# Attention and a squared-ReLU FFN on one core: who computes the low parts of x, a third buffer for the words of w_in, and three sums put off

## The chip, the cores and the metric

One core of a Trainium2 chip runs the whole kernel. The metric is device time in microseconds (us). A run is one execution; the time given is the median of three runs. The profile is of one further execution.

## The reference

```python
rmsnorm = lambda x, g: x / np.sqrt(np.mean(x * x, -1, keepdims=True) + 1e-6) * g
# q, k, v: (8, 12, 448, 64), float32
scores = 1 / np.sqrt(64) * np.matmul(rmsnorm(q, g_q), rmsnorm(k, g_k).transpose(0, 1, 3, 2))
attn = np.exp(scores - scores.max(-1, keepdims=True))
attn = attn / (attn.sum(-1, keepdims=True) + 1e-9)
x = np.matmul(attn, v).transpose(0, 2, 1, 3).reshape(3584, 768)
h = x @ w_in                      # w_in: (768, 2048), float64 in memory
r = np.maximum(h, 0.0)
out = (s * (r * r) + b) @ w_out   # w_out: (2048, 768), float64 in memory
```

## The kernel before, in words

**Two stages.** The first stage does the attention of all 8 batches and, beside it, the product x @ w_in with the ReLU. The second does the square, the affine step and the product with w_out, by a scheme of Strassen's kind with 7 products for each group of 256 tokens; `multiply(n)` is one product, 24 matmuls of 128x384, and `n = 7 * g + k` is its number for group `g`.

**Slots.** Two heads make a pair; there are 48 pairs, six to a batch. The order of the first stage is written by hand: the program walks through numbered slots, eight to a pair, 384 in all. In slot `s_` TensorE does the score tile that the exponential needs (`score_t`, tile `st`, two matmuls, L405 and L408), the score tile of ten slots later from which the row maxima are taken (`score`, tile `sh`, L367), and the product of the weights with v of two slots earlier (`weigh`, tile `av`, L464). Three `filler(2)` put six matmuls of x @ w_in (tile `ph`, L177) between them. A slot starts here with its L405 matmul. Work off TensorE is put into slots by `at(slot, function, ...)`; functions in the tuple `late` are recorded after the row maximum of the slot, the others before. Every engine then works through its own list in order, and so does SP, which issues all of the DMAs.

**Splitting.** Most matmul operands are split into a high part in the matmul's own type and a low part, the difference to it. `exponent` and `split_e` run on ScalarE, `split_e_lo` (tile `al`, or the upper half of `ah`) on VectorE. `split_kq` casts ka and qa on ScalarE and takes the differences (L351, L352) on GpSimd in the next slot; `scale` (L329 GpSimd, L330 VectorE) stands two slots ahead of it. `score` needs the new ka three slots after `split_kq` began.

**x and the boundary between batches.** When a pair is done, `divide` makes its tile `u` on GpSimd (L510). `split_x(b, g)` turns the six u of batch b into the tiles x0 to x5, high part on ScalarE (L517) and low part on VectorE (L518), one buffer per g. The matmuls of x @ w_in for batch b start at the end of slot 48(b+1)+8, so the slots around 48(b+1)+9 are called a boundary here; batch 0 has no such matmuls to run beside.

**Words of w_in.** w_in is loaded as 24 pieces of 512 float64 words (`load_piece`, tile `w64`, two buffers) and turned into single precision by five `convert` steps per piece on VectorE (L128 to L136), ScalarE (L129, L147) and GpSimd (L149). The tuple `PACE` gives the slot in which the conversion of each piece starts: every sixth slot up to 55, then every second or third up to 84. The second convert step is the last that reads the words.

**Second stage.** The seven combined blocks of w_out are loaded and split in chunks (`split_chunk`), the sums of the r tiles (`sum1` to `sum4`) and the splits of the operands (`split`) go to VectorE, and their tiles come from a list of free units.

Of the kernel before, what the change touches and what calls it, by code (L numbers as in the profile page):

```python
# [9 lines left out]
F32 = mybir.dt.float32  # L10
F32R = mybir.dt.float32r
I32 = mybir.dt.int32
AF = mybir.ActivationFunctionType
ALU = mybir.AluOpType
# [9 lines left out]
START = 9  # L24
# [9 lines left out]
TURNED = 10  # L34

PLAIN = 10

PACE_OUT = tuple(48 * b + 16 + 8 * i for b in range(2, 8) for i in range(4))

# [4 lines left out]
def attention_then_relu2_ffn(  # L44
# [29 lines left out]
    nc = tc.nc  # L74
    V, S, G, T = nc.vector, nc.scalar, nc.gpsimd, nc.tensor

    NPAIR, P, _, SEQ = kq.shape
# [5 lines left out]
    NP = NPAIR // B  # L83
    H = 2 * NP
    TILES = 2 * SEQ // P
    NV = PLAIN
    NQ = 4
    QC = SEQ // NQ
    REST = SEQ % P
    NCC = DM // P  # L90
# [5 lines left out]
    WI = 512  # L96
    NH = NFC // 2
    NQ3 = HALF // P
    W = 8
# [109 lines left out]
    with tc.tile_pool(name="apool", bufs=1) as ap:  # L209
        raws, kqs, invs, vrs, nmxs, shs, tks = ({} for _ in range(7))  # L210
        sts, movers, avs, uzs, zts, zbs, us = ({} for _ in range(7))
# [180 lines left out]
        def chunk(i):  # L392
            p, g = divmod(i, W)
            j, kc = divmod(g, NKC)
            return p, j, kc, P if kc < 3 or p < NV else REST
# [38 lines left out]
        def split_e_lo(i):  # L434
            p, j, kc, rows = chunk(i)
            if p < NV:
                return
            st, bank = sts.pop(i)
            ah = movers[i][0]
            if kc < 3:  # L440
                al = ap.tile([P, SEQ], F32R, tag="al", bufs=2, name=f"al{i}")
                movers[i].append(al)
            else:
                al = ah[rows:]
            V.tensor_tensor(al, st[:rows, :SEQ], ah[:rows].bitcast(F32), ALU.subtract)  # L445
            free.append(bank)
# [65 lines left out]
        xs = {}  # L512

        def split_x(b, g):
            u = us.pop(b * NP + g)
            x = xs[b, g] = xp.tile([P, 2, SEQ], F32R, tag=f"x{g}", name=f"x{b}_{g}")
            S.copy(x[:, 0, :], u)  # L517
            V.tensor_tensor(x[:, 1, :], u, x[:, 0, :].bitcast(F32), ALU.subtract)  # L518

        def pieces():  # L520
            for i, (hi, lo, src) in enumerate(parts_of_w_in()):
                w = ap.tile([P, WI, 2], I32, tag="w64", bufs=2, name=f"w64i{i}")


                def words(i=i):
                    return ap.tile([P, WI], I32, tag="wa", bufs=3, name=f"wai{i}")

                yield load_double((w, words, hi), hi, lo, src)
# [50 lines left out]
                    of.bitcast(F32).rearrange("p (k n) -> p k n", k=4),  # L579
                )  # L580

        late = (convert, invert, convert_out)

        fill = iter(())

# [8 lines left out]
        def at(s_, f, *a):  # L594
            jobs[s_].append((f, a))
# [31 lines left out]
            at(s0 + 18 - soon, divide, p, 3)  # L627
        for b in range(B):
            for g in range(NCC):
                at(W * NP * (b + 1) + START - 2 + g, split_x, b, g)  # L630
        for s_ in (-18, -10):
            at(s_, load_piece)
        for i, s_ in enumerate(PACE):
            for n in range(5):
                at(s_ + n, convert, i, n)
            at(s_ + 3, load_piece)
        for i, s_ in enumerate(PACE_OUT):
            at(s_ - 4, load_out, i)
            for n in range(5):
# [11 lines left out]
        with tc.manual_schedule(engines=ORDERED):  # L651
            begun = []
            for s_ in range(FIRST, NSLOT + START + NCC):
# [17 lines left out]
                for f, a in jobs[s_]:  # L671
                    if f in late:
                        continue
                    g = f(*a)
# [18 lines left out]
                b, m = divmod(s_ + 1 - START, W * NP)  # L693
# [7 lines left out]
    with tc.tile_pool(name="opool", bufs=1) as op:  # L701
# [17 lines left out]
        def release(*us):  # L719
            units.extend(tag for _, tag in us if tag is not None)  # L720
# [10 lines left out]
        def split_chunk(i):  # L731
            k, c = divmod(i, 4)
            hi, lo = (x[:, 2 * c : 2 * c + 2] for x in combs[k])
            S.copy(hi, lo.bitcast(F32))
            (G if k == 6 else V).tensor_tensor(lo, lo.bitcast(F32), hi.bitcast(F32), ALU.subtract)

        NG = NT // (2 * P)
        As = [{} for _ in range(NG)]
# [45 lines left out]
        def sum4(g):  # L784
            combine(g, 4, As[g][0, 1], As[g][2], ALU.subtract)

        USES = ((0, 0), (0, 1), 2, 1, 3, 4, (1, 1))
        def split(n):
            g, k = divmod(n, 7)
            if g == NG:  # L790
                return
            u = As[g].pop(USES[k])
            hi, lo = halves[n] = spare.pop(n) if n in spare else (unit(f"hi{n}"), unit(f"lo{n}"))
            S.copy(hi[0], single(u))  # L794
            V.tensor_tensor(lo[0], single(u), single(hi), ALU.subtract)  # L795
            release(u)

        banks = {}

# [53 lines left out]
        with tc.manual_schedule(engines=ORDERED):  # L853
            early = {
                2: [(load_a, 0, *c) for c in QUADS],
                6: [(f, 0, *c) for c in QUADS for f in (square, affine)],
                7: [*((f, 0) for f in (sum1, sum3, sum2, split, sum4)), (split, 1), (split, 2)],
                10: [(split, 3)],
            }
            splits = {**{m: 2 * m - 2 for m in range(1, 7)}, 8: 12, 9: 14, 12: 16, 13: 18}  # L860
            loads = {2: 2, 6: 3, 10: 4}
            for i in range(8):
                load_chunk(i)
            for m in range(NFC - 2):
                filler(NCC * 3)
                keep_r()
                if m in loads:
                    for i in range(4):
                        load_chunk(4 * loads[m] + i)
                if m in splits:  # L870
                    for i in range(2):
                        split_chunk(splits[m] + i)
                for f, *a in early.get(m, ()):
                    f(*a)
                rectify()
            filler(None)
            rectify()
            keep_r()
            units.extend(f"x{c}" for c in range(NCC))
            splits = {1: 20, 2: 22, 4: 24, 5: 26}  # L880
            loads = {0: 5, 3: 6}
            for n in range(7 * NG):
                g, k = divmod(n, 7)
                if n in loads:
                    for i in range(4):
                        load_chunk(4 * loads[n] + i)
                multiply(n)
                if n:
                    settle(n - 1)
                if n > 1:  # L890
                    split(n + 2)
                if n in splits:
                    for i in range(2):
                        split_chunk(splits[n] + i)
                if g + 1 < NG:
                    if k in (1, 2):
                        for c in QUADS[2 * k - 2 : 2 * k]:
                            load_a(g + 1, *c)
                    if k in (2, 3):
                        for c in QUADS[2 * k - 4 : 2 * k - 2]:  # L900
                            square(g + 1, *c)
                            affine(g + 1, *c)
                    if k == 3:
                        sum1(g + 1)
                    if k == 4:
                        sum3(g + 1)
                        sum2(g + 1)
                    if k == 5:
                        sum4(g + 1)
                release(*halves.pop(n))  # L910
            settle(7 * NG - 1)


# [42 lines left out]
```

## Time and profile before

| | |
|---|---|
| three runs | 1430.03, 1432.8, 1439.4 us, median 1432.8 |
| profiled execution | 1433.59 us, its span 1431.8 |
| TensorE busy | 1390.2 us, 97% |
| VectorE, ScalarE, GpSimd busy | 1058.1, 880.5, 655.7 us |
| granted TensorE clock, mean | 0.993 |

The span is counted from the first to the last instruction. A window is a stretch of the span; its row gives the busy time and the number of instructions of each engine. A row of the timeline gives the start, the time that it took, engine, line and operation, and in brackets how long the engine had been idle and for what it waited. SPq rows are DMA issues. A busy VectorE or GpSimd includes time in which an instruction has started but is held up.

### The profile page before, as it was taken

Reading aid. Unit: us, or ns where it says so; the run is one execution under the profiler, and the core shown is the slowest. Engines: PE = TensorE matmul, PEld = TensorE weight load, DVE = VectorE, ACT = ScalarE, POOL = GpSimd, SP = SyncE. Lnnn points to the kernel's source line nnn. Section 1 sums busy time; section 2 is a strip of 40 time slices with the busy share of each in tenths; the row PEclk is TensorE's granted clock in tenths of the full one; section 3 lists DMA queues with packets and bytes.
Section 4 is the critical chain, followed back from the end, with each engine's and each line's share of the span. In section 5 each row is a group of like instructions: output and inputs, shape, how many; then the busy total and the mean of one; then the engine's idle time right before and its main releaser. Section 6 shows DMA issues by size and latency. Waiting matters only on the chain.

```text
span 1431.8 us, 21377 instructions
## 1 busy us (share of the span) xinstructions
PE 1390.2 (97%) x7024; PEld 1269.3 (89%) x7024; DVE 1058.1 (74%) x1603; ACT 880.5 (61%) x1586; POOL 655.7 (46%) x515
## 2 busy tenths in 40 slices
PE   6998999999999999999999999999999999999999
PEld 5666778899899889989989988999999999999998
DVE  6898897788788778788878878734686567766673
ACT  4887567777777777777777767645643444334431
POOL 7777787677577757767756765300020000000000
PEclk8999999999999999999999999999999999999999
DMA  4455686688678768778767876438733342334330
GB/s 130 131 148 158 191 245 187 183 245 234 192 225 246 209 192 244 223 199 236 239 197 223 243 214 187 148 101 275 239 85 94 105 124 83 92 89 127 99 87 34
DMA packets 257470, 247.07 MB, mean 173 GB/s; under 512 B 77968, under 2 KB 238736, under 8 KB 257360
## 3 DMA queue, kind: packets, MB, share of 16 engines
q1 hardware_dynamic: 257360, 245.71, 58.9%
q8 instruction: 56, 0.92, 0.3%
q14 instruction: 54, 0.44, 0.1%
HBM read 180.88 MB, written 53.40 MB: 164 GB/s over the span
## 4 chain that ended last, share of the span: by engine, by line
PE 81%; DVE 7%; ACT 4%; DMA 3%; issue 3%; POOL 2%; SPq 0%; POOLq 0%; DVEq 0%; ACTq 0%
PE p L808 28%; PE ph L177 27%; PE av L464 12%; PE sh L367 4%; PE st L405 4%; PE st L408 4%; DMA w64i<-in_dram 2%; DVE x L518 1%; DVE nmx L378 1%; ACT x L517 1%; PE tk L245 1%; ACT st L424 1%; DVE al L445 1%; DVE kq L330 1%; DVE ah L445 1%
## 5 line engine op out<-in xcount | busy, mean ns | idle before, releaser
L177 PE MATMUL ph<-x,wih 128*128 128x448 f32 x1536 | 491.9, 367 | 0.1
L177 PEld LDWEIGHTS ph<-x,wih 128*128 128x128 f32 x1536 | 290.0, 189 | 27.8 <-issue 4.9
L177 PE MATMUL ph<-x,wil 128*128 128x448 f32 x768 | 290.6, 378 | 0.0
L378 DVE TENSOR_REDUCE nmx<-sh 112x1 fp32r<-112x448 f32 x384 | 236.4, 618 | 65.3 <-PE sh L367 61.9
L424 ACT ACTIVATE st<-st 128x448 f32<-128x448 f32 (+1 forms) x304 | 159.6, 525 | 195.1 <-PE st L408 191.3
L464 PE MATMUL av<-ah,vs 128*128 128x448 f32 x608 | 174.8, 369 | 2.5 <-DVE al L445 2.5
L367 PE MATMUL sh<-ka,qa 128*112 128x448 f32 x384 | 149.2, 391 | 24.1 <-DVE ah L445 10.4
L405 PE MATMUL st<-qa,ka 128*128 128x448 f32 (+1 forms) x384 | 159.5, 415 | 3.5 <-DVE nmx L378 3.4
L432 ACT CAST ah<-st 128x448 fp32r<-128x448 f32 (+1 forms) x304 | 161.9, 532 | 1.6
L177 PEld LDWEIGHTS ph<-x,wil 128*128 128x128 f32 x768 | 144.6, 188 | 16.5 <-issue 4.9
L445 DVE TENSOR_TENSOR al<-st,ah 128x448 fp32r<-128x448 f32 x228 | 139.2, 611 | 23.4 <-ACT ah L432 22.7
L351 POOL TENSOR_TENSOR ka<-kq,ka 64x448 fp32r<-64x448 f32 x76 | 102.6, 1351 | 102.0 <-ACT ka L348 98.5
L367 PEld LDWEIGHTS sh<-ka,qa 128*112 128x112 f32 x384 | 107.7, 281 | 38.4 <-DVE ah L445 12.3
L408 PE MATMUL st<-qb,kb 128*128 128x448 f32 (+1 forms) x384 | 141.1, 368 | 0.0
L464 PEld LDWEIGHTS av<-ah,vs 128*128 128x128 f32 x608 | 113.6, 189 | 15.6 <-DVE al L445 5.4
L794 ACT CAST hi<-a 128x1024 fp32r<-128x1024 f32 x54 | 56.8, 1052 | 87.5 <-PE p L808 71.8
L352 POOL TENSOR_TENSOR qb<-kq,qa 64x448 fp32r<-64x448 f32 x76 | 100.0, 1316 | 5.7
L329 POOL TENSOR_TENSOR kq<-kq,rb 128x448 f32<-128x448 f32 x76 | 101.0, 1329 | 0.0
L510 POOL TENSOR_TENSOR u<-uz,zb 128x448 f32<-128x448 f32 x48 | 64.7, 1347 | 79.2 <-DMA zb<-z_d 75.2
L313 POOL TENSOR_TENSOR ri<-ri,mhalf 128x14 f32<-128x14 f32 x38 | 99.3, 2614 | 3.2
L298 POOL TENSOR_TENSOR vs<-vr,vs 128x512 fp32r<-128x512 f32 x38 | 56.9, 1498 | 82.7 <-issue 73.9
L795 DVE TENSOR_TENSOR lo<-s,hi 128x1024 fp32r<-128x1024 f32 x41 | 50.1, 1223 | 52.5 <-ACT hi L794 52.5
(238 smaller groups left out, 3084.4 us busy)
## 6 DMA issues: line engine op xcount, KB each, us to landing
kq<-in_dram SPq DMA_DIRECT2D x76, 448.0 KB, 5.2
rb<-i_d SPq DMA_DIRECT2D x76, 448.0 KB, 6.0
r_d<-r SPq DMA_DIRECT2D x128, 224.0 KB, 3.5
a<-r_d SPq DMA_DIRECT2D x48, 512.0 KB, 5.2
raw<-in_dram SPq DMA_DIRECT2D x38, 448.0 KB, 4.8
w64i<-in_dram SPq DMA_DIRECT2D x24, 512.0 KB, 4.6
w64o<-in_dram SPq DMA_DIRECT2D x48, 256.0 KB, 3.6
kb<-ka SPq DMA_DIRECT2D x96, 112.0 KB, 2.6
```

The costliest lines, as they stand in the source:

```text
L177: T.matmul(ph[:, :SEQ], w[:, cc, f0 : f0 + P], xs[b, cc][:, part, :], start=cc == 0 and m == 0, stop=cc == NCC - 1 and m == 2,)
L329: G.tensor_tensor(t[:, 0], t[:, 0], rb[:, 0], ALU.mult)
L351: G.tensor_tensor(ka[n][D:, a], t[D:, 0], ka[n][D:, a].bitcast(F32), ALU.subtract)
L367: T.matmul(sh[:QC, :SEQ], qa[p % 2][:, a].rearrange("k (p c) -> k c p", c=NQ)[:, c], ka[p % 2][:, a], start=True, stop=True,)
L378: V.tensor_reduce(out=nmxs[p][:, c : c + 1], in_=sh[:QC, :SEQ], op=ALU.max, axis=AX.X, negate=True)
L405: T.matmul(st[:rows, :SEQ], ka[n][:, keys], qa[n][:, q], start=True, stop=False)
L408: T.matmul(st[:rows, :SEQ], kb[n][:, keys], qb[n][:, q], start=False, stop=True,)
L424: S.activation(st[:rows, :SEQ], st[:rows, :SEQ], AF.Exp)
L432: S.copy(ah[:rows], sts[i][0][:rows, :SEQ])
L445: V.tensor_tensor(al, st[:rows, :SEQ], ah[:rows].bitcast(F32), ALU.subtract)
L464: T.matmul(av[:, :SEQ], x, a, start=kc == 0 and m == 0, stop=kc == 3 and m == len(todo) - 1,)
L808: T.matmul(po, a[:, f], w[:, f], start=f == 0 and m == 0, stop=f == NH - 1 and m == 2,)
```

## The change

The low parts of x are computed by GpSimd for the batches after the first (VectorE still does them for batch 0) and are recorded late. The splits of x move two slots earlier (five slots, 5 to 9 of the next batch, and slot 11 for the last); for batch 0 the first five go to slots 20, 28, 36, 44 and 52. Pieces 13, 16 and 19 of w_in get a buffer of their own, whose room later holds the two low parts of the exponentials, in one tile named `low` in place of two buffers `al`. Loads of pieces stand one slot earlier, with one more load at slot 53. In the second stage the last block (k = 6) is split by VectorE in place of GpSimd, and sum2, sum4 and sum3 of group 1 stand after products 6, 6 and 7 in place of 4, 5 and 4. A scratch size for DMA descriptors is halved to 512.

```diff
+THIRD = (13, 16, 19)
@@ split_e_lo
-                al = ap.tile([P, SEQ], F32R, tag="al", bufs=2, name=f"al{i}")
+                if not lows:
+                    lows.append(ap.tile([P, 2, WI], F32R, tag="low", name="low"))
+                al = lows[0][:, kc % 2, :SEQ]
@@ split_x
-            u = us.pop(b * NP + g)
+            u = us[b * NP + g]
             x = xs[b, g] = xp.tile([P, 2, SEQ], F32R, tag=f"x{g}", name=f"x{b}_{g}")
             S.copy(x[:, 0, :], u)
-            V.tensor_tensor(x[:, 1, :], u, x[:, 0, :].bitcast(F32), ALU.subtract)
+
+        def split_x_lo(b, g):
+            u, x = us.pop(b * NP + g), xs[b, g]
+            (G if b else V).tensor_tensor(
+                x[:, 1, :], u, x[:, 0, :].bitcast(F32), ALU.subtract
+            )
@@ pieces
-                w = ap.tile([P, WI, 2], I32, tag="w64", bufs=2, name=f"w64i{i}")
+                if i in THIRD:
+                    w = ap.tile([P, WI, 2], I32, tag="low", name=f"w64i{i}")
+                else:
+                    w = ap.tile([P, WI, 2], I32, tag="w64", bufs=2, name=f"w64i{i}")
...
-        late = (convert, invert, convert_out)
+        late = (convert, invert, convert_out, split_x_lo)
...
-                at(W * NP * (b + 1) + START - 2 + g, split_x, b, g)
-        for s_ in (-18, -10):
+                s_ = W * NP * (b + 1) + START + (g - 4 if g < NCC - 1 else 2)
+                if b == 0 and g < NCC - 1:
+                    s_ = W * g + 20
+                at(s_, split_x, b, g)
+                at(s_, split_x_lo, b, g)
+        for s_ in (-18, -10, 53):
             at(s_, load_piece)
         for i, s_ in enumerate(PACE):
             for n in range(5):
                 at(s_ + n, convert, i, n)
-            at(s_ + 3, load_piece)
+            at(s_ + 2, load_piece)
@@ split_chunk
-            (G if k == 6 else V).tensor_tensor(lo, lo.bitcast(F32), hi.bitcast(F32), ALU.subtract)
+            V.tensor_tensor(lo, lo.bitcast(F32), hi.bitcast(F32), ALU.subtract)
...
+        held = {7: (0, 0), 8: (0, 1)}
@@ split
-            u = As[g].pop(USES[k])
+            u = As[g][USES[k]] if n in held else As[g].pop(USES[k])
...
-            release(u)
+            if n not in held:
+                release(u)
@@ loop over the products
+            put_off = {6: (sum2, sum4), 7: (sum3,)}
...
-                    if k == 4:
+                    if g > 0 and k == 4:
                         sum3(g + 1)
                         sum2(g + 1)
-                    if k == 5:
+                    if g > 0 and k == 5:
                         sum4(g + 1)
                 release(*halves.pop(n))
+                for f in put_off.get(n, ()):
+                    f(1)
+                    if f in (sum4, sum3):
+                        release(As[1].pop(held[8 if f is sum4 else 7]))
```

**GpSimd at the boundary after batch 1** (slots 101 to 108). `vs` and `ri` belong to v and to the norms, `kq`, `ka` and `qb` to the keys and queries of pairs ahead. Before:

```order
L298 TENSOR_TENSOR vs_2410<-vr_2706,vs_2410 128x4x2x64
L329 TENSOR_TENSOR kq_1_2761<-kq_1_2761,rb_1_2763 128x448
L312 TENSOR_SCALAR ri_2894<-ssq_2864 128x14
L313 TENSOR_TENSOR ri_2894<-ri_2894,mhalf 128x14
L351 TENSOR_TENSOR ka_186<-kq_1_2761,ka_186 64x448
L352 TENSOR_TENSOR qb_192<-kq_1_2761,qa_188 64x448
L510 TENSOR_TENSOR u_2987<-uz_2676,zb_2924 128x448
L329 TENSOR_TENSOR kq_0_2871<-kq_0_2871,rb_0_2873 128x448
L351 TENSOR_TENSOR ka_187<-kq_0_2871,ka_187 64x448
```

And now, from the second row of the same place:

```order
L331 TENSOR_TENSOR kq_1_2750<-kq_1_2750,rb_1_2752 128x448
L525 TENSOR_TENSOR x_0_2861<-u_1871,x_0_2861 128x448
L314 TENSOR_SCALAR ri_2882<-ssq_2850 128x14
L315 TENSOR_TENSOR ri_2882<-ri_2882,mhalf 128x14
L525 TENSOR_TENSOR x_1_2890<-u_2094,x_1_2890 128x448
L525 TENSOR_TENSOR x_2_2922<-u_2319,x_2_2922 128x448
L353 TENSOR_TENSOR ka_186<-kq_1_2750,ka_186 64x448
L354 TENSOR_TENSOR qb_192<-kq_1_2750,qa_188 64x448
L525 TENSOR_TENSOR x_3_2949<-u_2555,x_3_2949 128x448
L514 TENSOR_TENSOR u_2976<-uz_2667,zb_2914 128x448
L331 TENSOR_TENSOR kq_0_2857<-kq_0_2857,rb_0_2859 128x448
L525 TENSOR_TENSOR x_4_2984<-u_2772,x_4_2984 128x448
```

Three x stand ahead of the first ka and six ahead of the second (x_5 follows the last row shown, then ka_187).

**SP around slots 58 to 64.** w64i is a piece of w_in, z_d, zt and zb the division, qb and kb operands of the scores, kq and rb keys, queries and norms. Before, pieces 13, 14 and 15:

```order
L141 DMA w64i_1631<-in_dram 128x1024
L488 DMA zt_1514<-zr_1622 64x1x7
L285 DMA vf_1652<-in_dram 128x4x64 x2
L141 DMA w64i_1698<-in_dram 128x1024
L265 DMA kq_0_1721<-in_dram 128x2x448
L325 DMA rb_0_1723<-i_d_142 128x2x448
L500 DMA z_d_90<-zt_1514 128x7
L355 DMA qb_192<-nmx_1521 1x112x4
L355 DMA kb_191<-ka_187 64x448
L141 DMA w64i_1753<-in_dram 128x1024
```

Now, pieces 15 and 16:

```order
L492 DMA zt_1531<-zr_1632 64x1x7
L287 DMA vf_1657<-in_dram 128x4x64 x2
L143 DMA w64i_1674<-in_dram 128x1024
L267 DMA kq_0_1723<-in_dram 128x2x448
L327 DMA rb_0_1725<-i_d_142 128x2x448
L143 DMA w64i_1727<-in_dram 128x1024
L504 DMA z_d_90<-zt_1531 128x7
L357 DMA qb_192<-nmx_1538 1x112x4
L357 DMA kb_191<-ka_187 64x448
L209 DMA r_d_74<-r_0_1761 128x448
```

Ahead of the same z_d stand two pieces more than before; pieces 13 and 14 have moved out of the rows shown, to slots 53 and 57.

**VectorE at products 3 to 7 of the second stage.** comb62l is the low part of the last block, s and a_1_0 the sums of group 1, lo an operand's low part, o an output. Before:

```order
L795 TENSOR_TENSOR lo_11842<-a_1_1_11342,hi_11841 128x1024
L769 TENSOR_TENSOR a_1_0_11724<-a_0_0_11722,a_1_0_11724 128x1024
L772 TENSOR_TENSOR s_2_11850<-s_1_11812,a_0_0_11722 128x1024
L840 TENSOR_TENSOR o0a<-p_4_11814,o0a 128x384
L843 TENSOR_TENSOR o0d<-p_3_11778,o0a 128x384
L795 TENSOR_TENSOR lo_11882<-a_0_0_11722,hi_11881 128x1024
L772 TENSOR_TENSOR s_4_11889<-a_0_1_11766,s_2_11850 128x1024
```

Now:

```order
L813 TENSOR_TENSOR lo_11615<-a_1_1_11115,hi_11614 128x1024
L752 TENSOR_TENSOR comb62l<-comb62l,comb62h 128x768 x2
L859 TENSOR_TENSOR o0a<-p_4_11587,o0a 128x384
L862 TENSOR_TENSOR o0d<-p_3_11551,o0a 128x384
L813 TENSOR_TENSOR lo_11652<-a_0_0_11495,hi_11651 128x1024
L752 TENSOR_TENSOR comb62l<-comb62l,comb62h 128x768 x2
```

The four chunk splits stand where the three sums stood; the sums follow the splits of products 8 and 9.

More of the change, by code (lines that the diff above doesn't have):

```diff
@@ L514, in split_x @@
         def split_x(b, g):
-            u = us.pop(b * NP + g)
+            u = us[b * NP + g]
             x = xs[b, g] = xp.tile([P, 2, SEQ], F32R, tag=f"x{g}", name=f"x{b}_{g}")
             S.copy(x[:, 0, :], u)
-            V.tensor_tensor(x[:, 1, :], u, x[:, 0, :].bitcast(F32), ALU.subtract)
+        def split_x_lo(b, g):
[3 more added lines that the diff above has]
+            )
+        lows = []
         def pieces():
             for i, (hi, lo, src) in enumerate(parts_of_w_in()):
-                w = ap.tile([P, WI, 2], I32, tag="w64", bufs=2, name=f"w64i{i}")
+                if i in THIRD:
+                    w = ap.tile([P, WI, 2], I32, tag="low", name=f"w64i{i}")
+                else:
+                    w = ap.tile([P, WI, 2], I32, tag="w64", bufs=2, name=f"w64i{i}")
                 def words(i=i):
@@ L923 @@
     from concourse.bass_utils import run_bass_kernel_spmd as _run
-    nc = _bacc.Bacc("TRN2", target_bir_lowering=False, num_devices=1, dynamic_dma_scratch_size=1024)
+    nc = _bacc.Bacc("TRN2", target_bir_lowering=False, num_devices=1, dynamic_dma_scratch_size=512)
     k, q, v = (_np.asarray(inputs[n]) for n in ("k", "q", "v"))
```

## The prediction

> **What bounds the kernel now.** The first view is the page's table of busy time.
>
> ```profile
> PE 1390.2 (97%) x7024; PEld 1269.3 (89%) x7024; DVE 1058.1 (74%) x1603; ACT 880.5 (61%) x1586; POOL 655.7 (46%) x515
> ```
>
> TensorE is the bound. What a change outside it can bring lies in the 41.6 us in which TensorE isn't busy (1431.8 - 1390.2), and in stretches where its matmuls follow each other more slowly than they could. So the second view is windows, cut at slot starts and kept to L405, whose first column after the window is its length. A full window of this kind holds 16 slots (x17 where one reaches over an edge).
>
> ```profile
> 279.70:318.10 38.40, 5.88 (x16) 2.82 (x17) 1.00 0.81 240
> 237.80:279.70 41.90, 5.83 (x16) 2.76 (x16) 1.00 0.61 178
> 356.50:398.90 42.40, 5.89 (x17) 2.79 (x16) 1.00 0.64 187
> 475.60:519.00 43.40, 6.07 (x16) 2.90 (x16) 0.96 0.63 182
> 595.80:635.90 40.10, 5.86 (x16) 2.77 (x16) 1.00 0.70 198
> 712.70:754.70 42.00, 5.87 (x17) 2.79 (x16) 1.00 0.66 188
> 831.40:873.40 42.00, 5.86 (x16) 2.81 (x17) 1.00 0.65 189
> 122.80:195.40 72.60, 9.12 (x23) 4.61 (x24) 0.98 0.66 197
> 195.40:237.80 42.40, 5.88 (x17) 2.81 (x17) 1.00 0.70 207
> 152.30:180.60 28.30, 4.03 (x12) 2.08 (x12) 1.00 0.81 239
> ```
>
> The first row is an undisturbed stretch: 16 slots in 38.4 us, 2.40 a slot. The next six hold the boundaries after batches 1 to 6. Their excess over 38.4 is 3.5, 4.0, 5.0, 1.7, 3.6 and 3.6 us, **21.4 us** together. The next two are the stretch in which w_in is still being converted. Slots 57 to 79 take 72.6 us. The first ten pairs take their products with v in plain float32, so here the last row is the measure: 11 undisturbed slots in 28.3 us, 2.57 a slot. 23 of them would take 59.1 us, so **13.5 us** are excess; slots 80 to 95 have **4.0**. The third view is the waits of TensorE:
>
> ```profile
> PE sh L367 <- DVE ah L445: 10.4, 5, 2.1
> PE p L808 <- POOL comb62l L735: 1.6, 2, 1.4
> ```
>
> Five waits of 2.1 us are the boundaries; **1.6 us** belong to the second stage. Elsewhere the second stage has no gap, so it is at its floor.
>
> **The boundary, step by step.** From the timeline, VectorE and TensorE after batch 1:
>
> ```profile
> 255.33 0.37 PE L367 MATMUL sh<-ka,qa 128*112 128x448 f32 x1
> 257.08 1.62 DVE L518 TENSOR_TENSOR x<-u,x 128x448 fp32r<-128x448 f32 x1 [3.17 <-ACT x L517]
> 259.69 2.69 DVE L518 TENSOR_TENSOR x<-u,x 128x448 fp32r<-128x448 f32 x1
> 262.39 0.62 DVE L445 TENSOR_TENSOR ah<-st,ah 64x448 fp32r<-64x448 f32 x1
> 263.06 0.56 PE L367 MATMUL sh<-ka,qa 128*112 128x448 f32 x1 [2.08 <-DVE ah L445]
> ```
>
> VectorE first stands 3.17 us at x0, which is queued ahead of the exponentials' low parts and needs ScalarE's cast; then x0 and x1 take 1.62 and 2.69 us. The PSUM bank that ah frees at 263.0 comes late, and TensorE stands. GpSimd and ScalarE in that time:
>
> ```profile
> 252.86 1.16 POOL L329 TENSOR_TENSOR kq<-kq,rb 128x448 f32<-128x448 f32 x1
> 254.40 2.58 POOL L313 TENSOR_TENSOR ri<-ri,mhalf 128x14 f32<-128x14 f32 x1
> 257.06 1.16 POOL L351 TENSOR_TENSOR ka<-kq,ka 64x448 fp32r<-64x448 f32 x1
> 258.29 1.41 POOL L352 TENSOR_TENSOR qb<-kq,qa 64x448 fp32r<-64x448 f32 x1
> 259.66 1.15 POOL L510 TENSOR_TENSOR u<-uz,zb 128x448 f32<-128x448 f32 x1
> 260.77 1.12 POOL L329 TENSOR_TENSOR kq<-kq,rb 128x448 f32<-128x448 f32 x1
> 268.93 1.15 POOL L351 TENSOR_TENSOR ka<-kq,ka 64x448 fp32r<-64x448 f32 x1 [7.04 <-ACT ka L348]
> ```
>
> Both slow x start just after a GpSimd instruction and end some 0.5 us after it, or after two in a row (x1: past u and kq, to 262.4). The usual price is 0.6 us:
>
> ```profile
> L510 POOL TENSOR_TENSOR u<-uz,zb x48: 1134/1154/2216, 63.8 to 959.8; 128x448 f32<-128x448 f32 x48
> L517 ACT CAST x<-u x48: 547/562/576, 122.1 to 961.8; 128x448 fp32r<-128x448 f32 x48
> L518 DVE TENSOR_TENSOR x<-u,x x48: 606/626/2691, 122.9 to 962.7; 128x448 fp32r<-128x448 f32 x48
> ```
>
> The Trainium skill, "SBUF — State Buffer", section "Who interferes with whom", says that a VectorE instruction with two SBUF inputs and a GpSimd instruction that reads SBUF exclude each other for a whole instruction. The two rows agree (0.626 us against 2.69); by it the sum below would stay as it is.
>
> After the change none of this is on VectorE. On GpSimd an x isn't in the trace; u (L510) has its shape, two SBUF inputs and one output, so I take its median, 1.15 us, with 0.63 (VectorE's price) and 2.22 (u's longest) as ends. Does GpSimd keep up? From its rows: kq ends at 254.0, x0 at 255.2, ri with its power at 258.1, x1 and x2 at 260.4, ka at 261.6, where it ended at 258.2 before. Queued behind it is the sh matmul three slots after that of 255.33, due at 255.33 + 3 x 2.40 = 262.5. So the margin is 0.9 us, **tight**. Then qb 262.8, x3 264.0, u 265.1, kq 266.3, x4 and x5 268.6. The cast of that kq belongs to slot 107, whose sh is due at 255.33 + 4 x 2.40 = 264.9, so ScalarE stands there for 1 us or so; what is queued behind are the exponentials, which have more than a slot before their product. The second ka ends at 269.8, due at 255.33 + 7 x 2.40 = 272.1. The 7.04 us of idle time in the last POOL row is the room into which x4 and x5 fall. The x themselves are needed from slot 105 on, one a slot; each ends 2 us or more ahead of the sh of its slot. ScalarE has the same casts, two slots sooner.
>
> So the excess goes, but not all of it: the margin of 0.9 us will be missed at times, and the casts cluster on ScalarE. Of 21.4 us I count **-18** (from -21.4 to -9: half of it, if about 2 us of each 3.5 come back as a wait for ka).
>
> **Loads of w_in.** A window, and from the timeline around slot 61 the load of piece 13, SP's last issue ahead of a wait, ScalarE's wait for the piece, TensorE's for VectorE, and SP's next issue:
>
> ```profile
> 125.00:150.00 25.00, 19.24 (x76) 13.81 (x75) 19.89 (x33) 14.66 (x29) 16.00 (x12) 0.93 0.42 119
> 133.11 0.49 SPq L141 DMA_DIRECT2D w64i<-in_dram  x1
> 137.31 0.39 SPq L325 DMA_DIRECT2D rb<-i_d  x1
> 138.64 0.68 ACT L129 ACTIVATE wih<-w64i 128x512 fp32r<-128x512 f32 x1 [5.10 <-DMA w64i<-in_dram]
> 144.01 0.47 PE L405 MATMUL st<-qa,ka 128*128 128x448 f32 x1 [2.09 <-DVE nmx L378]
> 147.77 0.33 SPq L500 DMA_DIRECT2D z_d<-zt  x1
> ```
>
> Piece 13 is issued one slot ahead of its use and lands 5.5 us later; ScalarE stands 5.1 us, VectorE then waits for ScalarE, TensorE for VectorE, and the granted clock falls to 0.93 in these 25 us. SP stands too, 10.5 us at z_d. Now piece 13 is issued in slot 53, and the others five to six slots ahead of use in place of two, about 12 us against a landing of 5.5. Also, batch 0's six x leave VectorE in slots 55 to 60. Of the 13.5 us I count **-10** (from -13.5 to -2: VectorE's conversions themselves stay as they are, and they are dense here).
>
> Batch 0's x move into slots 20 to 52, whose slots are shorter. Five casts and differences, 5 x (0.56 + 0.63) = 6.0 us, if nothing hides them; nothing at all, if the idle time of both engines does. ScalarE gets the cast next to four others of the same slot, just ahead of an exponential; I take half, **+3**.
>
> **A new wait.** Piece 22 is issued in slot 76 into the buffer of piece 20, whose words are last read in slot 78. SP waits, and what is queued behind are kq and rb of slot 77, needed in slot 81. In the profile before:
>
> ```profile
> 189.43 0.60 SPq L265 DMA_DIRECT2D kq<-in_dram  x1
> 195.64 0.68 DVE L133 SCALAR_TENSOR_TENSOR wai<-w64i,wai 128x512 int32<-128x512 int32 x1
> 200.97 1.57 DVE L330 SCALAR_TENSOR_TENSOR kq<-kq,gqk,rb 128x448 f32<-128x448 f32 x1
> ```
>
> kq issued at 189.4, used at 201.0. If it goes only after L133 at 196.3 and takes the 5.5 us of the piece above, it lands at 201.8, 1 us late. Against it: VectorE runs less late without the waits for w64i. I take **+1** for slots 80 to 95 (from -3, most of their 4.0 of excess gone, to +7, the whole delay of the issue).
>
> **Second stage.** The last block, and a sum that it slows:
>
> ```profile
> 1038.39 10.21 POOL L735 TENSOR_TENSOR comb62l<-comb62l,comb62h 128x768 fp32r<-128x768 f32 x4 [77.49 <-ACT comb62h L734]
> 1041.29 2.87 DVE L769 TENSOR_TENSOR a<-a,a 128x1024 f32<-128x1024 f32 x1
> L735 DVE TENSOR_TENSOR comb5l<-comb5l,comb5h x4: 950/954/959, 1024.0 to 1029.3; 128x768 fp32r<-128x768 f32 x4
> ```
>
> Four chunks take 10.2 us on GpSimd and 3.8 (4 x 0.954) on VectorE, without the delay of the sums. The sums come after product 6; the operand from s_2 is first used three products later. The wait of 1.6 us goes: **-1.6** (from -1.6 to 0). The halved scratch and the tile `low` issue no instruction and cost nothing: low parts still alternate between two halves.
>
> **Sum** against the profiled execution's 1433.6 (1.8 more than its span, 0.8 above the median): -18 - 10 + 3 + 1 - 1.6 = -25.6, 1408.0; against the median, **1407**.
>
> **Rivals.**
> *GpSimd takes VectorE's place at the boundary.* TensorE then waits for ka and not for ah, 2 us at each. For it speak the margin of 0.9 us and that VectorE can hold GpSimd up in turn (qb took 1.41 us above, ka 1.16); against it the 7 us of idle time behind. The boundary gives -9 in place of -18, so 1416. The Trainium skill, "Perfetto Trace Analysis", section "Optimizing Scalar/DVE Operations", warns that moving work between these two engines might not help, as they share a read port. The trace agrees that they hold each other up, but in the rows above GpSimd has room and VectorE hasn't.
>
> *The loads don't help*, since VectorE's conversions bound slots 57 to 95 anyway and SP's new wait costs its +7: -18 - 2 + 3 + 7 - 1.6 = -11.6, which is 1421 against the median.
>
> *GpSimd's queue breaks, slower than before.* If each x takes the longest u, 2.2 us, ka of the first group ends 3 x 1.05 = 3.2 us later, 2.3 past due; the six together put the second kq and ka 4 us further back, and ScalarE with its casts. I make that 6 us a boundary in place of 3.6: +14 instead of -18, so 1439. It begins to cost more than now from about 1.9 us an x. Against it: u takes that long once or so in 48.
>
> *It does nothing*: the excess has another cause and the waits only change their names, 1433. The chain from x to ah to sh is too direct for much of that.
>
> **How the numbers follow.** My forecast has 0.70, the first rival 0.13, the loads 0.08, the broken queue 0.05, nothing 0.04. The forecast's own range comes from its ends, taken partly together: 1397 to 1418. To leave out no more than 2 in 10 the range reaches to the first two rivals: **1397 to 1421**. A measurement tells about 1%, 14 us, from no change. Below 1418.5 lie nearly all of the forecast, most of the first rival and a little of the second: faster 0.81; within 1% the rest of these and "nothing", 0.14; slower the broken queue, 0.05.
>
> **What would show it.** Right: windows with a boundary of 39 us instead of 42; no wait of sh for ah; no ACT L129 waiting 5 us around slot 61 and a granted clock of 1.00 there; no L808 waiting for comb62l; POOL's x near 1.15 us. Wrong: sh waiting for POOL's ka three slots after a boundary began; an idle SP between slots 76 and 78 followed by VectorE or GpSimd waiting for kq or rb; slots 16 to 56 longer by more than 6 us.

## The result: slower by 1%, and the profile after

The changed kernel takes 1446.4 us (median of six runs, 1443.4 to 1450.4) against 1431.7 of the kernel before on the same chip: a ratio of **1.0098** (95% interval 1.0069 to 1.0127). The forecast was 1407. The profiled execution took 1444.3 us, its span 1442.5. TensorE's row of the page:

```profile
PE 1395.9 (97%) x7024; PEld 1279.6 (89%) x7024; DVE 1036.6 (72%) x1565; ACT 882.3 (61%) x1586; POOL 687.9 (48%) x553
```

VectorE lost 21.5 us of busy time and GpSimd gained 32.2, as the change says; TensorE still stands 46.6 us (before 41.6), and its own busy time has grown by 5.7 us with the same number of matmuls. So I cut the span at the same slots as before and read the first column, the length. In order: slots 16 to 55, 56 to 79, 80 to 95, the stretch with the boundary after batch 1, an undisturbed one, and the other five boundaries. The last row is slots 16 to 55 of the kernel before.

```profile
53.40:138.50 85.10, 29.94 (x40) 8.11 (x41) 0.92 0.45 123
138.50:202.60 64.10, 9.40 (x24) 4.62 (x25) 1.00 0.67 200
202.60:246.80 44.20, 6.06 (x16) 2.90 (x17) 0.96 0.73 217
246.80:289.30 42.50, 6.09 (x16) 2.89 (x17) 0.96 0.62 182
289.30:327.70 38.40, 5.91 (x17) 2.79 (x16) 1.00 0.80 235
366.00:408.60 42.60, 6.09 (x16) 2.90 (x17) 0.96 0.66 193
485.30:527.90 42.60, 6.09 (x17) 2.91 (x17) 0.96 0.65 194
604.60:647.60 43.00, 6.12 (x17) 2.89 (x17) 0.96 0.66 190
724.30:766.80 42.50, 6.09 (x16) 2.85 (x16) 0.96 0.66 192
843.60:886.20 42.60, 6.11 (x17) 2.88 (x16) 0.96 0.66 193
54.40:121.50 67.10, 27.49 (x41) 7.56 (x41) 1.00 0.54 148
```

| stretch | before | after | difference | predicted |
|---|---|---|---|---|
| slots 16 to 55 | 67.1 | 85.1 | **+18.0** | +3 |
| slots 56 to 79 | 73.9 | 64.1 | -9.8 | -10 |
| slots 80 to 95 | 42.4 | 44.2 | +1.8 | +1 |
| six boundaries, excess over 38.4 | 21.4 | 25.4 | **+4.0** | -18 |
| from slot 383 to the end (second stage) | 486.1 | 484.1 | -2.0 | -1.6 |

With 1.0 us that the first slot begins sooner this is +11.0; the spans differ by 10.7 (1442.5 - 1431.8), so nothing of note is left over. Two terms are wrong, and both are waits of TensorE. Its waits in the changed kernel, and in the last two rows two of the kernel before (us in total, times, longest):

```profile
PE av L468 <- DVE low L449: 17.5, 9, 2.8
PE sh L369 <- DVE ka L259: 11.0, 5, 3.6
PE sh L369 <- ACT e L422: 4.9, 2, 2.5
PE sh L369 <- ACT uz L479: 2.6, 1, 2.6
PE av L464 <- DVE al L445: 6.2, 15, 1.3
PE sh L367 <- DVE ka L257: 5.8, 4, 3.6
```

The five waits of `sh` for `ah` have gone, as predicted, and so has the wait for comb62l. In their place `av` waits for `low`, the low part of the exponentials: six of the nine waits, 2.2 to 2.4 us each, are the six boundaries, and the longest is in slot 82. Five waits of `sh` are new, one each in slots 22, 30, 38, 46 and 54, of 2.4 to 2.7 us: two are put down to ka, two to e and one to uz.

**Slots 16 to 55.** Slots 22, 30, 38, 46 and 54 last 4.4 to 4.9 us, in place of about 2. From the timeline, ScalarE, GpSimd, VectorE and TensorE up to the wait in slot 22, sorted by start, and in the last row ScalarE's cast of the next x:

```profile
61.90 0.51 ACT L255 CAST ka<-tk 64x448 fp32r<-64x448 f32 x1
62.78 1.13 POOL L514 TENSOR_TENSOR u<-uz,zb 128x448 f32<-128x448 f32 x1
63.61 0.63 ACT L230 ACTIVATE sq<-rows 112x512 f32<-112x512 f32 x1
64.15 0.55 ACT L521 CAST x<-u 128x448 fp32r<-128x448 f32 x1
64.73 0.62 DVE L525 TENSOR_TENSOR x<-u,x 128x448 fp32r<-128x448 f32 x1 [2.28 <-ACT x L521]
65.98 0.62 DVE L259 TENSOR_TENSOR ka<-tk,ka 64x448 fp32r<-64x448 f32 x1
66.75 0.53 PE L369 MATMUL sh<-ka,qa 128*112 128x448 f32 x1 [2.67 <-DVE ka L259]
80.19 0.57 ACT L521 CAST x<-u 128x448 fp32r<-128x448 f32 x1 [0.30 <-POOL u L514]
```

On VectorE the low part of x stands ahead of the next pair's ka. It needs ScalarE's cast of x, and that stands on ScalarE behind the casts of ka and qa and the squares. VectorE is idle 2.28 us at x, and queued behind x is ka, for which ScalarE's cast was ready at 62.4 (61.90 + 0.51) and for which TensorE waits. But ScalarE's row isn't the only limit: u, from which the cast is made, was done only at 63.9 (62.78 + 1.13), 0.2 us before the cast began. At the five places u was done 0.03 to 0.44 us before the cast began, and at two of them ScalarE itself stood 0.3 us for it (last row). So with ScalarE's row empty the cast could have begun at most 0.4 us sooner.

**The boundary.** GpSimd does what the prediction listed: slot 96 starts 9.0 us later than before, and the two ka end at 271.0 and 279.6, where the list, moved by 9.0, has 270.6 and 278.8. TensorE doesn't wait for them. But VectorE's kq with two inputs (L332) meets GpSimd's next instructions. From the timeline, GpSimd and VectorE, and below them TensorE:

```profile
278.48 1.16 POOL L353 TENSOR_TENSOR ka<-kq,ka 64x448 fp32r<-64x448 f32 x1
279.72 1.17 POOL L354 TENSOR_TENSOR qb<-kq,qa 64x448 fp32r<-64x448 f32 x1
279.89 3.81 DVE L332 SCALAR_TENSOR_TENSOR kq<-kq,gqk,rb 128x448 f32<-128x448 f32 x1
280.83 1.30 POOL L300 TENSOR_TENSOR vs<-vr,vs 128x512 fp32r<-128x512 f32 x1
282.08 1.14 POOL L331 TENSOR_TENSOR kq<-kq,rb 128x448 f32<-128x448 f32 x1
283.62 0.61 DVE L449 TENSOR_TENSOR low<-st,ah 128x448 fp32r<-128x448 f32 x1
281.12 0.36 PE L369 MATMUL sh<-ka,qa 128*112 128x448 f32 x1
284.29 1.11 PE L468 MATMUL av<-ah,vs 128*128 128x448 f32 x2 [2.39 <-DVE low L449]
287.07 0.56 PE L179 MATMUL ph<-x,wih 128*128 128x448 f32 x1
```

kq usually takes 0.68 us. Here it starts just after qb and ends when qb, vs and GpSimd's kq are all done; `low` is queued behind it, and TensorE waits 2.39 us in slot 110. The stall has moved from slot 105, where VectorE's x made it, to slot 110. The last two rows tell the rest of the price: a matmul that took 0.36 us before the wait takes 0.56 for three us after it, and slots 110 and 111 together last 9.0 us in place of 4.9, which is the excess of 4.1.

One thing bears on the +4.0 itself. In the trace of before, TensorE waits for `ah` at five of the six boundaries, and the one after batch 4 has no such wait. The kernel "loads alone" below leaves x as it was before, waits at all six, and has an excess of 25.5. Against that, the changed kernel's 25.4 is no loss: the move exchanged one stall of some 4 us a boundary for another.

### The profile page after: what moved, and what is told of

Its sections match the earlier page's. It is cut to its first block, busy times and chain, and to the rows that moved or that the text cites. A ratio compares the mean times of both kernels' runs of the same rounds, so it can differ in the third digit from the quotient of the medians.

```text
span 1442.5 us, 21441 instructions
## 1 busy us (share of the span) xinstructions
PE 1395.9 (97%) x7024; PEld 1279.6 (89%) x7024; DVE 1036.6 (72%) x1565; ACT 882.3 (61%) x1586; POOL 687.9 (48%) x553
## 4 chain that ended last, share of the span: by engine, by line
PE 53%; DVE 1%; issue 1%; POOL 0%; DMA 0%; SPq 0%; ACT 0%; DVEq 0%; POOLq 0%
PE p L827 28%; PE ph L179 15%; PE av L468 5%; PE st L407 2%; PE st L410 2%; PE sh L369 2%; DVE kq L332 1%; DMA zt<-zr 0%; POOL x L525 0%; DVE low L449 0%; SPq L357 0%; POOL qb L354 0%; POOL kq L331 0%; POOL u L514 0%; ACT raw L306 0%
## 5 line engine op out<-in xcount | busy, mean ns | idle before, releaser
L468 PE MATMUL av<-ah,vs 128*128 128x448 f32 x608 | 175.9, 371 | 14.4 <-DVE low L449 14.4
L449 DVE TENSOR_TENSOR low<-st,ah 128x448 fp32r<-128x448 f32 x228 | 139.6, 612 | 38.5 <-ACT ah L434 37.0
L407 PE MATMUL st<-qa,ka 128*128 128x448 f32 (+1 forms) x384 | 162.6, 423 | 0.2 <-ACT e L422 0.2
L354 POOL TENSOR_TENSOR qb<-kq,qa 64x448 fp32r<-64x448 f32 x76 | 96.2, 1265 | 5.7
L332 DVE SCALAR_TENSOR_TENSOR kq<-kq,gqk,rb 128x448 f32<-128x448 f32 x76 | 93.8, 1234 | 2.5 <-DMA rb<-i_d 2.5
```

The costliest lines, as they stand in the source:

```text
L332: V.scalar_tensor_tensor(t[:, 1], t[:, 1], gqk, rb[:, 1], ALU.mult, ALU.mult)
L407: T.matmul(st[:rows, :SEQ], ka[n][:, keys], qa[n][:, q], start=True, stop=False)
L468: T.matmul(av[:, :SEQ], x, a, start=kc == 0 and m == 0, stop=kc == 3 and m == len(todo) - 1,)
```

## The experiments

All are edits of the changed kernel, but for one. The ratio is to the kernel before on the same chip (medians there 1435.1 to 1437.1 us); the stretches are from one profiled execution of each.

| kernel | ratio, 95% interval | slots 16-55 | 56-79 | 80-95 | boundaries' excess |
|---|---|---|---|---|---|
| before | 1 | 67.1 | 74.0 | 42.3 | 21.7 |
| the change | 1.0098 [1.0069, 1.0127] | 85.1 | 64.1 | 44.2 | 25.4 |
| batch 0 two slots later | 0.9994 [0.9969, 1.0018] | 68.8 | 68.2 | 49.3 | 25.9 |
| batch 0 on GpSimd | 0.9994 [0.9968, 1.0020] | 70.7 | 66.1 | 44.7 | 23.7 |
| two x on VectorE | 0.9907 [0.9880, 0.9934] | 86.7 | 63.4 | 50.3 | 0.6 |
| kq behind low part | 0.9923 [0.9902, 0.9944] | 85.1 | 62.8 | 46.2 | 6.6 |
| pieces 22, 23 later | 1.0054 [1.0023, 1.0084] | 86.8 | 64.1 | 42.9 | 23.4 |
| all x on VectorE, late | 0.9915 [0.9891, 0.9939] | 86.1 | 64.9 | 43.9 | 0.0 |
| loads alone (on before) | 1.0012 [0.9987, 1.0036] | 67.1 | 70.8 | 50.8 | 25.5 |
| three mends | 0.9826 [0.9796, 0.9856] | 68.8 | 68.1 | 41.2 | 1.2 |
| VectorE, late, old slots | 0.9915 [0.9889, 0.9940] | 86.6 | 63.0 | 43.6 | 2.4 |
| VectorE, sooner, early | 0.9954 [0.9930, 0.9978] | 90.4 | 63.7 | 43.9 | 5.7 |
| GpSimd, old slots | 0.9937 [0.9918, 0.9956] | 86.6 | 64.2 | 44.4 | 6.6 |
| VectorE x, pieces later | **0.9780** [0.9755, 0.9805] | 68.8 | 66.0 | 42.9 | 0.6 |

Stretches run from slot start to slot start and are rounded at the end, so that they can differ by 0.1 from the windows. Slots 80 to 95 vary between 41 and 51 us with where a held conversion of w_in falls, and are to be read with that in mind: the three kernels with some 50 us there (batch 0 two slots later, two x on VectorE, loads alone) are those whose profiled execution took 5 to 9 us more than their median, so these 50 us seem to belong to the execution shown.

### Batch 0: where its x stand

```diff
-                    s_ = W * g + 20
+                    s_ = W * g + 22
```

> The changed kernel with batch 0's first five x in slots 22, 30, 38, 46, 54 in place of 20, 28, 36, 44, 52; all else stays. Theory: in slot 20 the low part stands in VectorE's list ahead of ka and qb and waits over 2 us for a cast that ScalarE does behind four others; two slots later it stands in front of nothing urgent. The long slots of 4.4 to 4.9 us (22, 30, 38, 46, 54) fall to about 2, slots 16 to 55 are 14 to 17 us shorter, and the time is about 1431 us. Rival 1, the added work in short slots: five casts and differences are still there, so less than 4 us are won, 1443 or more. Rival 2, u comes too late: two slots later it is there, so this run gives the same as the theory.

The window of slots 16 to 55:

```profile
54.70:123.50 68.80, 27.48 (x40) 7.55 (x41) 1.00 0.53 142
```

16.3 us of the 18 are gone, with the same instructions two slots away from the cluster. So it is the place, not the added work. The shift gives both ScalarE's row and u more time, so it doesn't tell these two apart.

```diff
-            (G if b else V).tensor_tensor(
+            G.tensor_tensor(
```

> The changed kernel with batch 0's low parts on GpSimd too, slots unchanged. Theory: VectorE no longer stands at x, so ka and qb are on time; the cast stays where it was on ScalarE, 0.45 us ahead of an exponential. Long slots fall from 4.4-4.9 to 2.5 or less, 11 to 15 us won, about 1433 us. Rival 1, the added work: only VectorE's 0.6 us of each goes, 3 us won. Rival 2, u comes too late and ScalarE stands for it: nothing won, 1445.

```profile
54.90:125.60 70.70, 27.09 (x40) 7.55 (x40) 1.00 0.52 136
```

Here the casts stay at the bad place on ScalarE, and only VectorE no longer waits for them: 14.4 of the 18 us go, and 3.6 stay. So most of the cost is VectorE's wait, and not ScalarE's extra 0.55 us. Whether the cast for which VectorE waits is late through ScalarE's row or through u, no run shows.

### The boundary: who computes x

```diff
-            (G if b else V).tensor_tensor(
+            (G if b and g < 4 else V).tensor_tensor(
```

> The changed kernel with the low parts of x4 and x5 of batches 1 to 7 back on VectorE; x0 to x3 stay on GpSimd. Theory: GpSimd's unbroken row of qb, vs and kq after x5 is what holds VectorE's kq (3.8 us for an instruction of 0.7) in front of the exponentials' low part; without x4 and x5 GpSimd is 2.3 us ahead, has a gap there, and the wait in slot 110 goes. The windows of 16 slots with a boundary fall from 42.6 to about 39, 18 to 22 us won, about 1426 us. Rival, GpSimd is late as a whole since the three x ahead of the first ka: the wait stays to more than half, windows of 41 or more, 1437 or more.

```profile
254.40:292.80 38.40, 5.90 (x17) 2.79 (x16) 1.00 0.66 194
223.07 4.36 DVE L133 SCALAR_TENSOR_TENSOR wai<-w64i,wai 128x512 int32<-128x512 int32 x1
```

With x4 and x5 on VectorE, and two GpSimd instructions fewer ahead of slot 110, the boundary has no excess. The second row is the price of luck elsewhere: a conversion of w_in that usually takes 0.69 us was held 4.36 at slots 85 and 86, by GpSimd's qb, memsets, vs and kq in a row, and slots 80 to 95 lengthen to 50.3.

In the next kernel VectorE's kq gets a function of its own that is recorded late, behind the low part:

```diff
-        late = (convert, invert, convert_out, split_x_lo)
+        late = (convert, invert, convert_out, split_x_lo, scale_q)
...
                     at(s1 - 15, scale, p, j)
+                    at(s1 - 15, scale_q, p, j)
```

> The changed kernel with VectorE's scaling of q (kq, L332) recorded at the end of its slot, behind the exponentials' low part and the row maximum, in place of ahead of them; GpSimd's list is unchanged. Theory: kq is still held up by GpSimd for 2 to 4 us after the boundary, but nothing urgent stands behind it, so TensorE's wait for the low part in slot 110 falls from 2.4 to under 1 us; windows with a boundary 42.6 to 39 or 40, 12 to 20 us won, about 1430 us. Rival, GpSimd's lateness (second kq and ka, and ScalarE's cast 1.3 us late): no change, within 3 us of 1446.

TensorE's waits from 260 to 1000 us, and an instruction of VectorE in the first boundary's slot 110:

```profile
PE sh L372 <- POOL ka L356: 1.8, 6, 0.3
PE av L471 <- DVE low L452: 1.3, 6, 0.2
283.47 2.30 DVE L501 TENSOR_SCALAR zt<-zt 128x7 f32<-128x7 f32 x1
```

GpSimd is as full as before, but `low` isn't queued behind kq now: the wait of 2.4 us is 0.2. What is held instead is the next VectorE instruction in line, zt, 2.30 us for 0.15 at the same place of the changed kernel, and nothing urgent stands behind it. The 1.1 us left are the forecast's first rival in small: ka 0.3 us late.

```diff
-            (G if b else V).tensor_tensor(
+            V.tensor_tensor(
```

> The changed kernel with all low parts of x on VectorE, at the changed places (two slots sooner, behind the row maximum); GpSimd has none. Theory A (the boundary's stall is VectorE's two-input kq held by GpSimd working without a gap, and without x GpSimd has gaps): that wait of 3.8 us goes; x on VectorE take 0.6 to 2.7 us each, one a slot, but stand behind the exponentials' low parts, so the boundaries fall from 42.5 to 39 to 40 us, the same gain as with two x on VectorE or a little less: 1425 us or so. Theory B (x on VectorE is itself what stalls the boundary, as in the kernel before): windows of 41 to 42 us, as before the change, about 1436. Slots 16 to 56 keep their 85 us by both.

```profile
249.30:287.70 38.40, 5.91 (x17) 2.79 (x16) 1.00 0.70 200
```

No excess at all, and TensorE has no wait in any boundary. So x need not leave VectorE: another place on it was enough.

### Place in the slot, slot, engine

The next three take these apart. First, all on VectorE and late, at the slots of before; then at the changed slots, but not late; then on GpSimd at the slots of before. The edits:

```diff
-                s_ = W * NP * (b + 1) + START + (g - 4 if g < NCC - 1 else 2)
+                s_ = W * NP * (b + 1) + START + (g - 2 if b else 2)
...
-        late = (convert, invert, convert_out, split_x_lo)
+        late = (convert, invert, convert_out)
```

> The changed kernel with all low parts of x on VectorE, recorded late, and those of the batches after the first at the slots of before (two later than the change). Only the place within the slot differs from before at a boundary. Theory A (it is the place behind the row maximum that frees the boundary): boundaries of 38.4 to 39 us, about 1421. Theory B (it is the two slots): x0 and x1 meet the same GpSimd instructions as before and are held 1.6 to 2.7 us; boundaries of 41 to 43 us, about 1437. Slots 16 to 56 as in the change, 85 us.

> The changed kernel with all low parts of x on VectorE at the changed slots, but recorded with the first half of the slot as before (right behind their cast, ahead of the exponentials' low parts). Theory A (the place within the slot): VectorE stands up to 3 us for ScalarE's cast ahead of the low parts; boundaries of 40 to 43 us. Theory B (the two slots): 38.4 to 39 us. Slots 16 to 56, where batch 0's x stand the same way, may grow beyond 85 us by A, and stay by B.

> The changed kernel with x on GpSimd as in the change, but at the slots of before. If GpSimd working without a gap is what holds VectorE's two-input kq, the place of the six x among GpSimd's other instructions matters: two slots later x0 falls behind ri and the first ka, so a VectorE instruction of 3 us or more is held at another slot, and the boundaries stay between 41 and 43 us, about 1443. If only the particular slots of the change were bad, 38.4 to 39 us and about 1421. Slots 16 to 56 stay at 85 us.

One boundary window of each in this order (the second kernel's is the longest of its six, the others last 39.0 to 39.4 us), and TensorE's waits in the last kernel's boundaries:

```profile
248.90:287.90 39.00, 5.90 (x17) 2.79 (x16) 1.00 0.67 196
253.10:293.30 40.20, 5.89 (x17) 2.79 (x16) 1.00 0.63 192
250.70:290.10 39.40, 5.85 (x16) 2.77 (x16) 1.00 0.66 195
PE ph L179 <- POOL x L525: 3.7, 6, 0.6
```

Of 21.7 us of excess the place behind the row maximum alone leaves 2.4, the two slots alone 5.7, both together 0. On VectorE either of the two would have done most of it. The run that is not late lies between its two theories at the boundaries, and its slots 16 to 55 grew to 90.4 us, as the first of them said. GpSimd at the old slots leaves 6.6, and there the x themselves come 0.6 us late; at the changed slots it leaves 25.4. My expectation for that run, 41 to 43 us by the rule that a full GpSimd always holds VectorE's kq long, was wrong: kq was held there too, but 1.69 us only, and `low` was in time.

### The loads of w_in and SP's wait

The loads part alone, put into the kernel before:

```diff
+THIRD = (13, 16, 19)
...
-        for s_ in (-18, -10):
+        for s_ in (-18, -10, 53):
...
-            at(s_ + 3, load_piece)
+            at(s_ + 2, load_piece)
```

> The kernel before with the loads of w_in alone changed: third buffer, tile low, loads a slot earlier, one more at slot 53, the scratch halved; x, the last block and the sums as before. Theory A (the 9.8 us that the changed kernel gained in slots 56 to 79 come from the loads): slots 56 to 79 about 64 to 65 us, 80 to 95 about 44 (SP's new wait), slots 16 to 56 67 us, the boundaries 40 to 43 as before, so about 8 us less than before: 0.994. Theory B (a good part of it came from batch 0's x leaving VectorE in slots 55 to 60): slots 56 to 79 stay at 68 us or more, and the whole within 0.3% of before.

Slots 56 to 79 and 80 to 95, and from the timeline ScalarE at slot 57 and VectorE at slot 86:

```profile
122.40:193.20 70.80, 9.79 (x25) 4.77 (x25) 0.98 0.64 192
193.20:244.00 50.80, 6.26 (x16) 2.96 (x16) 0.90 0.63 189
123.92 0.95 ACT L306 ACTIVATE raw<-raw 128x896 f32<-128x896 f32 x1 [2.74 <-DMA raw<-in_dram]
212.76 4.35 DVE L133 SCALAR_TENSOR_TENSOR wai<-w64i,wai 128x512 int32<-128x512 int32 x1
```

The waits of 5 us for w64i are gone (slots 61 to 63 take 9.6 us, before 15.4), but ScalarE now waits for `raw`, and slots 57 and 58 last 11.7 in place of 8.1. So the loads alone are worth 3.2 us there. In the execution shown slots 80 to 95 take more than that back (its span of 1442.0 is one of its longer ones); the median, 1435.0, is even with before.

```diff
-            at(s_ + 2, load_piece)
+            at(s_ + (5 if i == 19 else 4 if i >= 20 else 2), load_piece)
```

> The changed kernel with the load of piece 22 two slots later and that of piece 23 two slots later too (piece 21's place is kept), so that neither stands on SP in wait for its buffer ahead of kq and rb of slot 77; all else as changed. Theory A (the excess of slots 80 to 95 is SP's wait at piece 22): VectorE's and GpSimd's waits of 2.5 and 4.3 us for rb go, slot 82 falls from 6.1 us to about 2.4, and slots 80 to 95 from 44.2 us to 40 or less, so the whole to about 4 us less than the change, 1.007 against before. Theory B (it is VectorE's two-input instruction of a conversion or of kq, held while GpSimd works without a gap): the waits for rb go, and a slot of 5 us or more stays somewhere in 80 to 95, with a VectorE instruction of 3 us or more ahead of it; 43 to 46 us. Slots 16 to 56 (85 us) and the boundaries (42.5 us each) don't move by either.

```profile
206.30:249.20 42.90, 5.91 (x17) 2.79 (x16) 0.96 0.69 203
211.76 2.35 DVE L135 SCALAR_TENSOR_TENSOR wai<-w64i,wai 128x512 int32<-128x512 int32 x1
```

The waits for rb are gone and slot 82 falls from 6.1 to 4.6 us, but the stretch gains only 1.3 us: VectorE's conversions are held one after the other there (1.3 to 2.4 us each) beside a GpSimd without a gap. Each theory had one half of it.

### The edits together

Batch 0 two slots later, two x on VectorE, and the pieces as in the last edit:

> The changed kernel with three edits together: batch 0's x two slots later (slots 22, 30, 38, 46, 54), two of the six x of the other batches back on VectorE, pieces 22 and 23 loaded two slots later. If the terms add, as they should when each has its own place: slots 16 to 56 about 69 us (16 less than the change), the boundaries 38.4 (25 less in all), slots 80 to 95 between 40 and 46; together about 40 us less than the change, so some 1403 us on the profile's basis of before at 1433.6, a ratio of 0.978 to 0.985. Rival: the terms overlap (slots 80 to 95 grow to 50 us, as they did with each of the first two edits), 1410 to 1415.

```profile
122.50:190.60 68.10, 9.64 (x25) 4.67 (x25) 1.00 0.73 220
125.15 0.95 ACT L306 ACTIVATE raw<-raw 128x896 f32<-128x896 f32 x1 [3.82 <-DMA raw<-in_dram]
SPq L143 <- DVE wai L135: 7.8, 4, 3.7
```

0.9826, within the range expected, where the change has 1.0098. The last row is from SP's waits at 95 to 140 us: with loads a slot sooner SP stands at a piece's buffer, and the load of raw behind it is late. The last kernel has all x on VectorE and gives each piece its old slot:

```diff
-            at(s_ + 2, load_piece)
+            at(s_ + (5 if i == 19 else 4 if i >= 20 else 3), load_piece)
```

> The best of the runs so far and two edits more: all low parts of x on VectorE (late, at the changed slots), batch 0's two slots later, each piece of w_in loaded a slot later than in the change (as before the change), pieces 22 and 23 at slots 79 and 81 as above. Expected: boundaries 38.4, slots 16 to 56 about 69 us, slots 56 to 79 three us below the 68.0 of the kernel with three mends, if what made its slot 57 last 6.6 us is the load of raw that SP issues only after a wait of 3.7 us for a piece's buffer; slots 80 to 95 about 41; together 1400 us, a ratio of 0.978 to 0.982. Rival: raw isn't sooner or slot 57 has another cause, and it is the same as with three mends, 0.983.

```profile
122.40:188.40 66.00, 9.62 (x25) 4.63 (x25) 1.00 0.73 221
```

ScalarE's wait for raw falls from 3.8 to 0.8 us, slot 57 from 6.6 to 4.4, the stretch by 2.1 where I expected 3. At **0.978** (median 1404.9 us) it beats both kernels.

## Why the prediction was wrong, point by point

- **The boundary, -18 forecast, +4 measured.** Right: the wait of `sh` for `ah` and its cause, GpSimd's new timeline, that sh isn't late. The step that failed is the sentence on the rule for two SBUF inputs, "by it the sum below would stay as it is", and with it "none of this is on VectorE": VectorE's kq has two SBUF inputs and stayed. I had asked only whether GpSimd's own results come in time, and called GpSimd's "7 us of idle time" the room for x4 and x5. That gap it took from VectorE's kq. The rivals had GpSimd late or its queue broken; none had VectorE held by it. Keeping all else and moving `low` ahead of kq cuts the excess to 6.6 us, and taking two x out of GpSimd's row to 0.6, so both halves of the mechanism are shown.
- **Batch 0, +3 forecast, +18 measured.** The term was sized as work, "five casts and differences, 6.0 us, if nothing hides them", and half of that. The text even names the four casts beside it. It should have counted the wait: VectorE's x is recorded in the slot of the cast that it needs, that cast stands behind four ScalarE instructions and needs a u that is only just done by then, and ka is behind x. At each of the five places VectorE waits 2.1 to 2.5 us and TensorE 2.4 to 2.7, and slower matmuls follow (the window's clock is 0.92): 3.6 us each (18.0 / 5). Two slots' shift shows that it is the place; which of the two makes the cast late stays open.
- **Slots 56 to 79, -10 forecast, -9.8 measured**: right in size, and only partly for the reason given, so the size is partly luck. The loads alone are worth 3.2. With batch 0's x gone from slots 55 to 60 as well, it is 5.7 (73.9 to 68.2). The rest appears only in kernels whose slots 16 to 55 are long: slots 16 to 79 together take 136.8 to 137.0 us in all three kernels without the stall of batch 0 and with the loads at the changed slots, however it was mended. That the longer slots let SP and GpSimd get ahead of slot 57 fits this, but no run tested it by itself.
- **Slots 80 to 95, +1 forecast, +1.8 measured.** The reason given is there, and without it (pieces 22 and 23 later) the stretch is 1.3 us shorter. But the ten kernels with these loads take 43.6 to 50.8 us there, so that the number is so close is luck. From the changed kernel's timeline, SP's issue behind piece 22, and the two that wait for it:

```profile
204.25 0.59 SPq L327 DMA_DIRECT2D rb<-i_d  x1
211.30 0.69 DVE L332 SCALAR_TENSOR_TENSOR kq<-kq,gqk,rb 128x448 f32<-128x448 f32 x1 [2.50 <-DMA rb<-i_d]
211.37 1.61 POOL L331 TENSOR_TENSOR kq<-kq,rb 128x448 f32<-128x448 f32 x1 [4.25 <-DMA rb<-i_d]
```

- **Second stage, -1.6 forecast, -2.0 measured.** comb62l takes VectorE 0.954 us a chunk, and TensorE no longer waits for it.

- **That the low parts of x should leave VectorE** the prediction took over from the change without asking. They need not: it was enough to record them behind the exponentials' low parts, on the engine on which they were.

## What to carry to other kernels

Before work goes to another engine, try it in another place of the same engine's list: here the place alone removed 19 of 21.7 us, place and slot together all of it, and the move to GpSimd on top of them brought 25 back. When an engine's list is filled up, ask not only whether its own results come in time but which instructions of the other engine used its gaps, and what is queued behind those. And size an added instruction by the wait at its head and by what is behind it in line, not by its duration: 0.6 us of work cost 3.6 us each time.

## What the runs showed of the hardware

- A VectorE instruction with two SBUF inputs was held not by one GpSimd instruction but by three or four in a row (kq 3.81 us for 0.68, L133 4.36 for 0.69). With an instruction more or less in GpSimd's row it got in after two (1.69 us). The Trainium skill, "SBUF — State Buffer", section "Who interferes with whom", says that whichever of the two issues first has the port for its whole instruction and that the other blocks until then; the rows agree on the blocking, but the 3.81 us are longer than one instruction of GpSimd (1.30 at most here). Which of the two is next when GpSimd has its next instruction ready wasn't told apart.
- It also held a VectorE instruction on 7 columns with one tensor input (zt, 2.30 us for 0.15 in the changed kernel), and it did so at all six boundaries of that kernel (2.30 to 2.33).
- A wait of TensorE of 2.4 us cost 4.1: matmuls took 0.56 us in place of 0.36 for some three us after it, and the granted clock of the window fell to 0.96. Boundaries with a wait of 0.6 us (GpSimd at the old slots) kept 1.00 and lost 1.1.
